# Where the key and value loads of a decode kernel land: a turning ring of eighteen slots against two whole-head places

## The chip, the cores and the metric

The kernel runs on one core of one Trainium2 chip. The metric is device time in microseconds (us) of one execution, lower is better. The kernel before takes 1354.32 us (median of 3 runs, 1352.16 to 1354.4). The trace that is read here is of one more execution, whose own time was 1351.85 us; from its first to its last instruction the profile counts a span of 1349.9 us.

Five engines work beside each other: TensorE (PE in the profile, its weight loads PEld), VectorE (DVE), ScalarE (ACT), GpSimd (POOL) and SyncE (SP). SP does no arithmetic here; it issues the transfers of keys and values. ACT issues those of most weights. A transfer is carried out by 16 DMA engines, and a transfer of 128 rows gives each of them eight packets and then a short one that tells the semaphore.

## The reference: one token, two layers, a long cache

The same weights and the same cache serve both layers. Everything is float32.

```python
# x: 1 x 640; k_cache, v_cache: 32 heads x 8192 x 128; wq: 640 x 4096; wo: 4096 x 640
# w1: 640 x 1728; w2: 1728 x 640
x = x + attention(layernorm(x))   # q = x wq; p = softmax(q k^T / sqrt(128)); (p v) wo
x = x + relu(layernorm(x) w1) w2
x = x + attention(layernorm(x))
x = x + relu(layernorm(x) w1) w2
```

There is one query, so each layer reads the whole cache: 32 heads of 8 MB (4 MB of keys and 4 MB of values), and does little with each byte.

## The kernel before: heads in a row, a ring for their loads

**The ring.** One tile, `ring`, holds whatever of the cache is on the chip: `RING` = 4760 units of 32 bytes in each of the 128 partitions, 4 KB over all of them. A piece of keys (a quarter of a head's keys, `K_ALL`) or of values (`V_ALL`) takes 256 units, which is 1 MB. A head is four pieces of keys and four of values: 2048 units, 8 MB. Head 0 has nine, since its last piece of values is cut in halves, so that little work is left when the last one lands.

**The list of loads.** `todo` is a list of (layer, unit, first piece, piece behind the last, place), written when the program is built. `pump` (called at the start, and by `release` after each piece has been used) takes loads from its head in order, as long as the place wanted is free of live pieces (`is_free`), or, where no place is given, as long as `place` finds a gap that fits. Each load is one `nc.sync.dma_start` (L210). So all loads of keys and values stand in one line on SP: a load that waits for its place holds up those behind it, and on the chip SP waits until TensorE has read the last old piece that the new load covers.

**Places.** In the first layer heads run from 0 to 31, in the second from 31 to 0. Some pieces of heads 29 to 31 stay on the chip from the first layer to the second (`KEPT` = 3960 units) and are not loaded twice. Heads 2 to 26 (`FULL`) are stored as one unit of keys and values. `turning` walks them around 18 slots of 256 units (`SLOTS`): a head takes the next eight slots, and where the ring of 18 ends within a head, the head is loaded in two loads, one up to the end and one from slot 0. Of its 48 heads (25 in the first layer, 23 in the second) 31 are whole and 17 divided: 2 and 6 slots, 4 and 4, or 6 and 2. The other loads have their own cuts: in the first layer head 0 is six loads and head 1 four; in the second layer heads 26 and 25 are two each (keys, values), head 1 four, head 0 six. The four blocks of `w2` come last in each layer, through `place`.

**The work of a head.** `scores` (L454) multiplies the query with the key pieces on TensorE, 32 matmul records a head; `row_maxima` (L465, DVE) and `exponentials` (L470 PE, L477 DVE, L479 ACT exp, L483 and L485 DVE) make the weights, and `values` (L503) multiplies them with the value pieces, 32 records again. `output` (L518 to L533) sums the rows. Each piece is released as soon as its own matmuls are done, so keys are free some 7 us before values. In between lie side jobs: the next group's queries (L393 to L417), the projection with `wo` (L425), the folding of the last `wo` rows into `w1` (L569 to L604). In the second layer the first three heads are interleaved (`AHEAD`). TensorE takes everything in the written order: a head's matmuls wait for its pieces and hold up the next head's.

**The end of a layer.** Before the last head's values are done, the rest is projected (`before_last`) and the first part of the MLP (`hidden`, L609) runs between its pieces; then come the sums (L547), the last part of `hidden`, the turn of its result (L825 to L841) and the product with `w2` (L425 within `times_rows`).

The functions as the diff touches them:

Of the kernel before, what the change touches and what calls it, by code (L numbers as in the profile page):

```python
# [17 lines left out]
H = 32  # L18
# [15 lines left out]
RUN = COLS // 4  # L34
NBL = RUN // P
K_ALL = [(r, 0, RUN) for r in range(4)]
V_ALL = [(b, 0, 4) for b in range(NBL)]
WHOLE = [("k", K_ALL), ("v", V_ALL)]
HALVES = [("k", K_ALL[:2]), ("k", K_ALL[2:]), ("v", V_ALL[:2]), ("v", V_ALL[2:])]
LAST = [("v", V_ALL[:2]), ("v", V_ALL[2:3]), ("v", [(3, 0, 2)]), ("v", [(3, 2, 2)])]  # L40
FULL = range(2, 27)
UNITS = {h: [("kv", K_ALL + V_ALL)] if h in FULL else WHOLE for h in range(H)}
UNITS[0] = HALVES[:2] + LAST
UNITS[1] = HALVES
UNITS[28] = HALVES
UNITS[29] = [
    ("k", K_ALL[:1]),
# [9 lines left out]
]  # L57
UNITS[30] = [
    ("k", [(0, 432, 80), (1, 0, 80)]),
    ("k", [(0, 0, 432)]),  # L60
    ("k", [(1, 80, 432)] + K_ALL[2:]),
] + HALVES[2:]
UNITS[31] = HALVES[:2] + LAST
DROPPED = {29: 9, 30: 2}
# [3 lines left out]
AHEAD = 3  # L68


SLOT = RUN // 2
SLOTS = 18


def kind_of(unit, t):

    return unit[0] if unit[0] != "kv" else "k" if t < len(K_ALL) else "v"


def wide(kind, piece):  # L80

    if kind == "w":
        return D // 8
    return 4 * piece[2] * (1 if kind == "k" else DH) // 8
# [13 lines left out]
W2_ALL = [("w2", i) for i in range(len(W2_RUNS))]  # L98
# [4 lines left out]
def decode_kernel(ctx: ExitStack, tc: tile.TileContext, x, kv, wq, wo, w1, w2, w2_rest, out):  # L103
# [15 lines left out]
    kept = [u for u in order if u[0] >= min(DROPPED) and u[1] >= DROPPED.get(u[0], 0)]  # L119
# [3 lines left out]
    todo = []  # L123

    def all_of(layer, u):
        todo.append((layer, u, 0, len(UNITS[u[0]][u[1]][1]), None))

    def turning(layer, heads, slot):

        for h in heads:  # L130
            a, end = 0, len(UNITS[h][0][1])
            while a < end:
                b = min(end, a + SLOTS - slot)
                todo.append((layer, (h, 0), a, b, SLOT * slot))
                slot = (slot + b - a) % SLOTS
                a = b

    for h in range(H):
        if h == FULL[0]:
            turning(0, FULL, 16)  # L140
        if h not in FULL:
            for i in range(len(UNITS[h])):
                all_of(0, (h, i))
    for u in W2_ALL:
        all_of(0, u)
    for h in range(H)[::-1]:
        if h == FULL[-1]:
            todo.append((1, (h, 0), 0, len(K_ALL), None))
            todo.append((1, (h, 0), len(K_ALL), len(K_ALL) + len(V_ALL), None))
            h = FULL[-2]  # L150
            todo.append((1, (h, 0), 0, len(K_ALL), 0))
            todo.append((1, (h, 0), len(K_ALL), len(K_ALL) + len(V_ALL), SLOT * len(K_ALL)))
            turning(1, FULL[:-2][::-1], 8)
        if h not in FULL and h != 30:
            for i in range(len(UNITS[h])):
                if (h, i) not in kept:
                    all_of(1, (h, i))
    for u in W2_ALL:
        all_of(1, u)
    source = {}  # L160
    for us, dram in ((order, kv), (W2_ALL, w2)):
        o = 0
# [7 lines left out]
    def place(layer, u, n):  # L170

        step = 512 if n % 512 == 0 else 8
        if layer:
            low, high = 0, RING
        elif u[0] in range(FULL[0]):
            low, high = 0, 16 * SLOT
        elif u[0] == "w2":
            low, high = KEPT, RING
        elif u in apart:
            low, high = apart[u]  # L180
        else:
            low, high = 0, 3072
        at, best = low, None
        for a, m in sorted(live.values()) + [(high, 0)]:
            a = min(a, high)
            for base in (0, 3328, KEPT):
                c = base + -(-max(at - base, 0) // step) * step
                if a - c >= n and (best is None or a - at < best[1]):
                    best = c, a - at
            at = max(at, a + m)  # L190
        return None if best is None else best[0]
# [4 lines left out]
    def pump():  # L196
        while todo:
            layer, u, first, last, at = todo[0]
            unit = UNITS[u[0]][u[1]]
            ns = [wide(kind_of(unit, t), piece) for t, piece in enumerate(unit[1])]  # L200
            n = sum(ns[first:last])
            if at is None:
                at = place(layer, u, n)
                if at is None:
                    return
            elif not is_free(at, n):
                return
            todo.pop(0)
            o = 8 * sum(ns[:first])
            nc.sync.dma_start(ring[:, 8 * at : 8 * (at + n)], source[u][:, o : o + 8 * n])  # L210
            for t in range(first, last):
                live[layer, u, t] = at, ns[t]
                at_of[layer, u, t] = ring, 8 * at
                at += ns[t]
# [759 lines left out]
```

## Time and profile before

| what | value |
|---|---|
| median of 3 runs | 1354.32 us (1352.16 to 1354.4) |
| the profiled execution's own time | 1351.85 us |
| its span, first to last instruction | 1349.9 us |
| PE busy | 787.8 us (58%) |
| DVE busy | 251.6 us (19%) |
| ACT busy | 59.1 us (4%) |
| bytes moved by DMA | 574.52 MB, 426 GB/s over the span |
| loads of keys and values with no size shown | 31 |

Busy time of an engine is the union of its instructions. The DMA share is the mean busy share of the 16 DMA engines. "us to landing" of a load runs from its issue on SP until all 16 engines have told its semaphore, so it includes the time in which the load stood behind earlier ones. The chain of waits is followed back from the last instruction: at each step to what released it.

### The profile page before, as it was taken

What the parts mean: (1) busy time and instruction counts of PE and PEld (TensorE: products, weight loads), DVE (VectorE), ACT (ScalarE), POOL (GpSimd) and SP (SyncE); (2) the same over time, 40 slices, a digit from 0 to 9 for tenths busy, and PEclk for the clock granted to TensorE, in tenths of its full rate; (3) what the DMA queues carried; (4) which work ended last, traced back from release to release, by engine and by line L of the source; (5) the groups of instructions that cost most, each with busy time, mean ns of one, the idle gap of its engine ahead of it and who ended that gap; (6) DMA issues with size and microseconds to landing.
All of it is one profiled execution on the core that took longest, in us unless ns stands there. A gap on an engine that the chain in (4) does not pass through costs nothing.

```text
span 1349.9 us, 13614 instructions
## 1 busy us (share of the span) xinstructions
PE 787.8 (58%) x6080; PEld 268.6 (20%) x6080; DVE 251.6 (19%) x794; ACT 59.1 (4%) x149; POOL 2.9 (0%) x10
## 2 busy tenths in 40 slices
PE   5454555554755655566588664575466554665658
PEld 2011111111211211121143211122122121211214
DVE  2111111221211211122122211122111111112212
ACT  0000000000000000000000000000000000000000
POOL 0000000000000000000000000000000000000000
PEclk8677677868878876789799877788778778878879
DMA  9999999999999999999999999999999999999997
GB/s 395 438 428 441 423 430 442 425 427 430 439 429 429 432 434 422 447 416 420 426 382 425 435 430 438 424 436 429 436 435 427 426 438 429 434 421 438 429 422 317
DMA packets 25409, 574.52 MB, mean 426 GB/s; under 512 B 2820, under 2 KB 2952, under 8 KB 6024
## 3 DMA queue, kind: packets, MB, share of 16 engines
q1 hardware_dynamic: 20600, 531.15, 91.7%
q10 hardware_dynamic: 4752, 42.52, 7.5%
q8 instruction: 47, 0.77, 0.2%
q14 instruction: 10, 0.08, 0.0%
HBM read 573.65 MB, written 0.00 MB: 425 GB/s over the span
## 4 chain that ended last, share of the span: by engine, by line
DMA 66%; PE 27%; DVE 5%; issue 1%; ACT 1%; ACTq 0%; SPq 0%; DVEq 0%
DMA ring<-in_kv 65%; PE ps L454 13%; PE outs L503 8%; DVE h_t L465 2%; PE px L393 1%; DVE pt L483 1%; PE pm L470 1%; ACT p L479 1%; DVE p L522 1%; PE acc L425 0%; PE px L425 0%; PE acc L609 0%; PE px L408 0%; DVE pT L485 0%; DMA ring<-in_w 0%
## 5 line engine op out<-in xcount | busy, mean ns | idle before, releaser
L454 PE MATMUL ps<-ring,spread_q 128*32 128x512 f32 (+3 forms) x2104 | 326.2, 767 | 337.7 <-DMA ring<-in_kv 332.4
L503 PE MATMUL outs<-ring,pT 128*4 128x512 f32 (+1 forms) x2080 | 260.6, 642 | 32.8 <-DVE pT L485 17.5
L454 PEld LDWEIGHTS ps<-ring,spread_q 128*32 128x32 f32 x2104 | 76.2, 137 | 523.2 <-issue 298.9
L465 DVE TENSOR_REDUCE h_t<-ps 128x1 f32<-128x512 f32 x64 | 44.3, 692 | 637.1 <-PE ps L454 637.1
L479 ACT ACTIVATE p<-ps,h_t 128x512 f32<-128x512 f32 x64 | 44.0, 687 | 1227.3 <-DVE h_t L477 1207.6
L503 PEld LDWEIGHTS outs<-ring,pT 128*4 128x4 f32 x2080 | 51.6, 91 | 181.8 <-issue 149.4
L532 PE MATMUL pm<-ones,p 128*128 128x1 f32 x120 | 23.2, 262 | 94.9 <-DVE p L522 94.9
L518 DVE TENSOR_SCALAR p<-outs,ind 128x128 f32<-128x128 f32 x60 | 21.1, 351 | 246.4 <-PE outs L503 246.4
L522 DVE SCALAR_TENSOR_TENSOR p<-outs,ind,p 128x128 f32<-128x128 f32 x180 | 63.1, 351 | 6.4
L483 DVE STREAM_TRANSPOSE pt<-p 128x512 f32<-128x512 f32 x64 | 46.5, 727 | 58.2 <-ACT p L479 58.2
L470 PE MATMUL pm<-row_of,h_t 128*128 128x16 f32 x128 | 26.3, 281 | 50.0 <-DVE h_t L465 49.0
L532 PEld LDWEIGHTS pm<-ones,p 128*128 128x128 f32 x120 | 18.0, 190 | 152.1 <-DVE p L522 150.8
L470 PEld LDWEIGHTS pm<-row_of,h_t 128*128 128x128 f32 x128 | 20.0, 196 | 110.1 <-DVE h_t L465 108.2
L596 PE MATMUL px<-w_t,wct 128*128 128x448 f32 (+1 forms) x80 | 35.1, 553 | 1.1 <-ACT wct L589 1.1
L393 PE MATMUL px<-wq_t,ln_xc 128*32 128x256 f32 x280 | 34.3, 393 | 0.0
L492 PE MATMUL pm<-ind,h_t 128*128 128x1 f32 x128 | 22.6, 246 | 15.3 <-ACT p L479 15.3
L492 PEld LDWEIGHTS pm<-ind,h_t 128*128 128x128 f32 x128 | 22.1, 198 | 33.3 <-ACT p L479 27.0
L425 PE MATMUL acc<-wo_t,o_cols 128*32 128x160 f32 x496 | 21.5, 313 | 0.6 <-DVE o_cols L550 0.6
L533 DVE TENSOR_SCALAR o_cols<-pm,h_t 128x1 f32<-128x1 f32 x60 | 13.1, 219 | 30.5 <-PE pm L532 30.5
L393 PEld LDWEIGHTS px<-wq_t,ln_xc 128*32 128x32 f32 x280 | 15.7, 113 | 13.7 <-issue 2.9
L477 DVE TENSOR_REDUCE h_t<-pm 128x1 f32<-128x16 f32 x64 | 11.2, 175 | 33.1 <-PE pm L470 33.1
L425 PEld LDWEIGHTS acc<-wo_t,o_cols 128*32 128x32 f32 x496 | 15.0, 113 | 3.9 <-issue 1.5
(110 smaller groups left out, 203.4 us busy)
## 6 DMA issues: line engine op xcount, KB each, us to landing
ring<-in_kv SPq DMA_DIRECT2D x20, 4096.0 KB, 35.5
ring<-in_kv SPq DMA_DIRECT2D x38, 2048.0 KB, 28.5
ring<-in_kv SPq DMA_DIRECT2D x11, 6144.0 KB, 37.7
wq_t<-in_wq ACTq DMA_DIRECT2D x14, 1280.0 KB, 25.0
wo_t<-in_wo ACTq DMA_DIRECT2D x14, 1280.0 KB, 25.6
ring<-in_kv SPq DMA_DIRECT2D x15, 1024.0 KB, 12.7
ring<-in_w SPq DMA_DIRECT2D x4, 1280.0 KB, 26.9
w_t<-in_w ACTq DMA_DIRECT2D x1, 4320.0 KB, 49.3
```

The costliest lines, as they stand in the source:

```text
L393: nc.tensor.matmul(pq[32 * j : 32 * j + 32, :n], xc[:, c : c + 1].to_broadcast([P, 32]), wq_t[g][:, c, j * n : (j + 1) * n], start=(c == 0 ...
L425: nc.tensor.matmul(acc[32 * g : 32 * g + 32, :DR], col.to_broadcast([col.shape[0], 32]), wt[:, g * DR : (g + 1) * DR], start=first, stop=last,
L454: nc.tensor.matmul(hd.ps[32 * g : 32 * g + 32, c : c + n], spread_q[:, 3 - r : 35 - r], tile_of[:, at + g * n : at + (g + 1) * n], start=f ...
L465: nc.vector.tensor_reduce(hd.nm, hd.ps, AX.X, ALU.max, negate=True)
L470: nc.tensor.matmul(pt[:, :16], hd.nm.to_broadcast([P, P]), row_of.rearrange("p g r -> p (g r)"), start=True, stop=True,)
L479: nc.scalar.activation(hd.p, hd.ps, AF.Exp, bias=hd.low, scale=1.0, accum_out=hd.l)
L483: nc.vector.transpose(pt, hd.p)
L492: nc.tensor.matmul(pt[:, :1], hd.l.to_broadcast([P, P]), ind[:, 4:5], start=True, stop=True)
L503: nc.tensor.matmul(hd.out[32 * g : 32 * g + 4, r : r + m].rearrange("p r d -> p (r d)"), hd.pT[:, 4 * i : 4 * i + 4], tile_of[:, v : v + m ...
L522: nc.vector.scalar_tensor_tensor(oc[:, r], hd.out[:, r], ind[:, r : r + 1], oc[:, r - 1], op0=ALU.mult, op1=ALU.add,)
L532: nc.tensor.matmul(pt[:, :1], oc[:, 3], ones, start=True, stop=True)
L596: nc.tensor.matmul(pt[:, :n], wct[:, c], w1_t[:, c, f : f + n], start=(c == 0), stop=(c == NB - 1),)
```

## The change: two places, whole heads

Heads 0 to 26 become one unit each. `turning` and the 18 slots go. `parts_of` gives a head one of two places of 2048 units: the first layer's even heads have place 0 and its odd heads place 2048, the second layer's odd heads place 0 and its even heads place 2048 (head 26 of the second layer goes wherever `place` finds room, as before). A head is one load, except where `PARTS` cuts it: head 0 of the first layer as keys, then values; in the second layer heads 26, 25 and 2 as keys, then values, head 1 in four loads and head 0 in six. Loads of heads 27 to 31 and of `w2` are listed as before, but their places are found among other live pieces. Units 4096 to 4760 hold nothing of heads 2 to 26 any more. What the engines compute, and in which order, stays the same: the pieces are the same and are used in the same order.

```diff
-UNITS = {h: [("kv", K_ALL + V_ALL)] if h in FULL else WHOLE for h in range(H)}
-UNITS[0] = HALVES[:2] + LAST
-UNITS[1] = HALVES
+UNITS = {h: [("kv", K_ALL + V_ALL)] if h <= FULL[-1] else WHOLE for h in range(H)}
+UNITS[0] = [("kv", K_ALL + V_ALL[:3] + [(3, 0, 2), (3, 2, 2)])]
+PARTS = [{0: [4, 9]}, {26: [4, 8], 25: [4, 8], 2: [4, 8], 1: [2, 4, 6, 8], 0: [2, 4, 6, 7, 8, 9]}]
...
-SLOT = RUN // 2
-SLOTS = 18
+HALF = 4 * RUN
...
-    def turning(layer, heads, slot):
-
-        for h in heads:
-            a, end = 0, len(UNITS[h][0][1])
-            while a < end:
-                b = min(end, a + SLOTS - slot)
-                todo.append((layer, (h, 0), a, b, SLOT * slot))
-                slot = (slot + b - a) % SLOTS
-                a = b
...
+    def parts_of(layer, h):
+
+        ((kind, pieces),) = UNITS[h]
+        ns = [wide(kind_of((kind, pieces), t), piece) for t, piece in enumerate(pieces)]
+        at = None if (layer, h) == (1, FULL[-1]) else HALF * (h % 2 != layer)
+        a = 0
+        for b in PARTS[layer].get(h, [len(pieces)]):
+            todo.append((layer, (h, 0), a, b, at))
+            if at is not None:
+                at += sum(ns[a:b])
+            a = b
+
+    for layer in range(2):
+        for h in range(H)[:: 1 - 2 * layer]:
+            if h <= FULL[-1]:
+                parts_of(layer, h)
+            elif not layer or h != 30:
+                for i in range(len(UNITS[h])):
+                    if not layer or (h, i) not in kept:
+                        all_of(layer, (h, i))
+        for u in W2_ALL:
+            all_of(layer, u)
...
-        elif u[0] in range(FULL[0]):
-            low, high = 0, 16 * SLOT
```

More of the change, by code (lines that the diff above doesn't have):

```diff
@@ L126, in all_of @@
         todo.append((layer, u, 0, len(UNITS[u[0]][u[1]][1]), None))
-    def turning(layer, heads, slot):
-        for h in heads:
-            a, end = 0, len(UNITS[h][0][1])
-            while a < end:
-                b = min(end, a + SLOTS - slot)
-                todo.append((layer, (h, 0), a, b, SLOT * slot))
-                slot = (slot + b - a) % SLOTS
-                a = b
[L138 to L159, printed above, removed]
+    def parts_of(layer, h):
[18 more added lines that the diff above has]
+            all_of(layer, u)
     source = {}
```

## The prediction, made before the changed kernel had run

> **What bounds the kernel now.** I read the page's lines on DMA first, then the busy time in the two long stretches between the layers' ends, then the chain of waits.
>
> ```profile
> span 1349.9 us, 13614 instructions
> ...
> DMA  9999999999999999999999999999999999999997
> ...
> q1 hardware_dynamic: 20600, 531.15, 91.7%
> q10 hardware_dynamic: 4752, 42.52, 7.5%
> ...
> DMA 66%; PE 27%; DVE 5%; issue 1%; ACT 1%; ACTq 0%; SPq 0%; DVEq 0%
> ```
>
> ```profile
> 30.00:670.00 640.00, 357.24 (x2582) 114.25 (x2574) 113.22 (x341) 25.48 (x64) 0.00 (x0) 0.78 1.00 430
> 725.00:1325.00 600.00, 346.99 (x2596) 115.26 (x2592) 113.56 (x344) 26.63 (x67) 0.00 (x0) 0.82 1.00 431
> ```
>
> The second fence's columns are the stretch, its length, busy time (count) of PE, PEld, DVE, ACT and POOL, the granted clock, the DMA share and GB/s. For 1240 of the 1349.9 us the DMA engines have a share of 1.00. PE works little over half of that time. So in the long stretches nothing can be won by loading earlier. What is left is the time that a byte takes on the DMA engines, and the places where something else sets the end.
>
> One such place is the end of the kernel, seen in the chain of waits:
>
> ```profile
> 1266.69 28.31 DMA ring<-in_kv
> 1295.00 0.04 issue
> 1295.05 5.82 PE ps L454 x32
> ...
> 1304.19 3.66 PE outs L503 x32
> ...
> 1317.31 3.66 PE outs L503 x32
> ...
> 1336.06 0.92 PE outs L503 x14
> 1336.98 0.02 issue
> ...
> 1347.35 0.01 DVEq L968
> ```
>
> The last landing on the chain is that of the second layer's head 2, whole, at 1295.00. From there 52 us of PE, DVE and ACT follow: heads 2, 1 and 0, then the MLP. The loads behind head 2 land before they are wanted.
>
> **Fewer loads.** The groups of DMA issues show today's sizes; whole heads are the 31 for which no size is given.
>
> ```profile
> ring<-in_kv SPq DMA_DIRECT2D x20, 4096.0 KB, 35.5
> ring<-in_kv SPq DMA_DIRECT2D x38, 2048.0 KB, 28.5
> ring<-in_kv SPq DMA_DIRECT2D x11, 6144.0 KB, 37.7
> ...
> ring<-in_kv SPq DMA_DIRECT2D x31, 31.9
> ```
>
> By the lists, heads 0 to 26 are 6 + 4 + 34 = 44 loads in the first layer today and 2 + 26 = 28 after. In the second they are 2 + 2 + 31 + 4 + 6 = 45 and then 2 + 2 + 22 + 2 + 4 + 6 = 38. That is 16 and 7 loads fewer, 23 in all, with the same bytes. What does one more load cost where the DMA engines are full? Two places without weight loads tell, the chain of waits in the second layer and TensorE's timeline of the first layer's head 1:
>
> ```profile
> 756.47 36.34 DMA ring<-in_kv
> ...
> 798.31 33.27 DMA ring<-in_kv
> ```
>
> ```profile
> 35.71 3.64 PE L454 MATMUL ps<-ring,spread_q 128*32 128x512 f32 x16 [1.92 <-DMA ring<-in_kv]
> 40.60 1.92 PE L454 MATMUL ps<-ring,spread_q 128*32 128x512 f32 x16 [1.25 <-DMA ring<-in_kv]
> 45.89 2.85 PE L503 MATMUL outs<-ring,pT 128*4 128x512 f32 x16 [0.64 <-DVE pT L485]
> 50.39 3.43 PE L503 MATMUL outs<-ring,pT 128*4 128x512 f32 x16 [1.65 <-DMA ring<-in_kv]
> ```
>
> From 792.81 (756.47 + 36.34) to 831.58 (798.31 + 33.27) land head 25 in two loads and head 24 in one: 16 MB and 3 loads in 38.77 us. From 35.71 to 50.39, where PE starts on landings, come 6 MB in 3 loads: 14.68 us. With b us for a MB and a for a load, 16b + 3a = 38.77 and 6b + 3a = 14.68, so b = 2.409 and a = 0.075 us. The page gives a second, rougher reading: q1's share is 0.917 x 16 x 1349.9 = 19806 engine-us for 20600 packets and 531.15 MB, q10's 1620 for 4752 and 42.52; the two solve to 0.011 us a packet, and a load has nine per engine, so 0.10 us. I take 0.075, since landings include what overlaps, with 0.05 and 0.10 as ends. 23 loads are 1.73 us (1.2 to 2.3): 1.2 before the first layer's end, 0.5 in the second.
>
> The Trainium skill, "DMA: Bandwidth & Descriptors", section "Measured (HBM→SBUF, 128 partitions, SWDGE, issued from GpSimd)", gives about 10.5 ns a packet, for another way of issuing. Nine packets a load and 23 loads would be 2.2 us by it; the landings say 1.73 and decide.
>
> **Less room ahead.** Today a load of 2 to 6 slots can go while the head before last is still in work, since 18 slots are 2.25 heads, and a head that crosses no end waits only for the last old piece under its slots. With two places head h+2 goes when the last values of head h are read, and then only head h+1 stands in the queue. It takes 38.77 / 2 = 19.4 us. The queue runs dry if head h's work and the start of a load together take longer. The slow heads are those with side jobs or a low clock; head 7 of the first layer is one, in PE's timeline:
>
> ```profile
> 188.00 6.33 PE L454 MATMUL ps<-ring,spread_q 128*32 128x512 f32 x32 [10.21 <-DMA ring<-in_kv]
> ...
> 197.71 6.57 PE L503 MATMUL outs<-ring,pT 128*4 128x512 f32 x32 [0.59 <-DVE pT L485]
> ```
>
> From landing to the last value matmul that is 204.28 - 188.00 = 16.3 us. How long a load takes from its issue to its first bytes isn't shown, but a bound is, since a small load (320 KB, itself under 0.8 us at 2.4 us a MB) lands so soon after its issue:
>
> ```profile
> wct<-in_kv SPq DMA_DIRECT2D x1, 320.0 KB, 2.9
> ```
>
> 16.3 + 2.9 = 19.2 us, under 19.4, and the heads with side jobs are also those beside which 1280 KB weight loads run, which lengthen the cover by some 3 us each. So the cost here is nothing; what hides it is head h+1's transfer, and without that cover a load would cost up to 2.9 us of gap each. SP has nothing else behind these waits but later loads of the ring: weights go through ACT's queue. Head 0, as keys then values, holds its place until its values are done, some 3 us later than today, while head 1's 19.4 us run.
>
> The thinnest cover is moved, not made: the second layer's head 25 today gets its keys in when head 27's scores are done, and after the change when head 26's are, at 788.98, which is when its values go today.
>
> ```profile
> 788.98 10.14 SPq L210 DMA_DIRECT2D ring<-in_kv  x3
> ```
>
> What stands before it lands at 792.81: 3.8 us, above the bound of 2.9. At the first layer's end head 27's values likewise wait for head 26's scores, with head 27's keys in the queue (9.7 us). Nothing again.
>
> **Head 2 as keys, then values.** Its keys will land some 9.7 us before its values, so scores and exponentials run beside the values' transfer, and after the landing near 1295 only 3.66 us of value matmuls are left instead of the 12.8 us to 1307.85. The chain at the end gets 9 us of slack, far more than it can use: the loads of heads 1 and 0 become what is late next. How much that gives, the landings of head 0 say:
>
> ```profile
> 1298.75 0.33 SPq L210 DMA_DIRECT2D ring<-in_kv  x1
> ```
>
> ```profile
> ring<-in_kv SPq DMA_DIRECT2D x1, 2048.0 KB, 26.4
> ```
>
> ```profile
> 1306.20 0.38 SPq L210 DMA_DIRECT2D ring<-in_kv  x1
> ```
>
> ```profile
> ring<-in_kv SPq DMA_DIRECT2D x1, 512.0 KB, 29.3
> ```
>
> The second half of its keys lands at 1325.15 and the last piece of values at 1335.5. The first layer's end is already paced by these same loads, and shows the way from keys to the end of the values:
>
> ```profile
> 660.26 22.56 DMA ring<-in_kv
> ...
> 692.41 1.04 PE outs L503 x16
> ```
>
> That is 682.82 to 693.45, 10.6 us. In the second layer, with everything 1.73 us earlier: keys 1323.4, so values done at 1334.05; the last values land at 1333.8 and need some 0.5 us, 1334.3. The later holds, rounded to 1334.5 for waits between. Today it is 1336.98. **Sum:** 1336.98 - 1334.5 = 2.5 us at the end, which contains the 1.73 of the loads; 0.8 is the chain's share. The span goes from 1349.9 to 1347.4 and the profiled execution from 1351.85 to 1349.35. That execution was 2.5 us under the median of the runs, so against 1354.32 the forecast is **1351.8 us**. Own range: 1.2 to 3.7 less, 1350.6 to 1353.1.
>
> **The rivals.** *The clock falls at the end, so that only little is won.* Paced by loads, PE works and waits by turns. Against it: the first layer's end, paced the same way, keeps the clock at 1.00. For it: head 1's start in the first layer, also fed by 2048 KB loads, has 0.72, and 16 matmuls took 1.92 us at one place and 3.43 to 3.64 at others.
>
> ```profile
> 676.00:694.00 18.00, 15.35 (x154) 5.98 (x147) 3.67 (x12) 1.17 (x4) 0.00 (x0) 1.00 1.00 418
> ...
> 36.00:55.00 19.00, 12.34 (x68) 2.21 (x60) 2.99 (x9) 0.78 (x2) 0.00 (x0) 0.72 1.00 426
> ```
>
> Slow keys and values of head 0 add 1.7 us for the last two key pieces, and about as much again until PE has worked for a while: 2 us off the gain, 1353.8 us. The Trainium skill, "TensorE: Matmul & The Clock Gate", section "HAM oscillation — how this bites in real kernels", has the clock halved after PE gaps of more than about 3.4 us, which speaks against this change; the gaps of 1.25 and 1.65 us above stand beside slow matmuls already, so the trace is, if anything, harsher.
>
> *More is won.* Were a load 0.10 us (2.3 in all) and the values' end bound by landings alone, 1.4 us more: 3.7 less, 1350.6 us. The page's rounder reading speaks for it, the landings against.
>
> *The queue runs dry* (the slower side). If the heads with side jobs, one in four of 52, took head 1's 18.1 us (35.71 to 53.82, its waits for pieces included) and a load's start its whole 2.9, each would leave 21.0 - 19.4 = 1.6 us empty: 13 x 1.6 = 21 us, 1373 us. It decides from 16.5 us of work on. Against it: 16.3 is the longest I found among whole heads, and weight loads run then.
>
> *It doesn't do what it says*: head 2's keys wait for its old place longer than the queue lasts, so no split is felt: 1.73 less, 1352.6. Head 4's scores free it some 19 us ahead; unlikely.
>
> **How the numbers follow.** Forecast 0.43; clock 0.27; more 0.12; dry 0.13; no effect of the split 0.05. A measurement tells about 0.2%, 2.7 us, from no change. The forecast lies at 0.19%, so half of it, with nearly all of "more" and a little besides, is faster: 0.38. The other half, the clock case and the last make 0.47; dry makes most of 0.15. The range goes from 1349.3 (more, and 1.3 for the scatter of medians) to 1357.0, which takes in the clock case with a colder end and a queue that runs dry by 0.4 us a time.
>
> **What would show it.** The DMA share must stay at 1.00 from 30 to 670 and from 725 to 1325; q1 must have 23 x 144 = 3312 packets fewer, about 17290. Whole heads' landings must be 19.4 us apart where no weights run. The chain at the end must go through a landing of head 0, not head 2, and the clock from 1320 on must be 1.00. A share under 0.99, or PE waits for landings longer than 19.4 us behind SP waits for values, would make me wrong on the side of slower.

## The result and the profile after

| | before | changed |
|---|---|---|
| median | 1353.63 us (1351.57 to 1356.14, 22 executions) | 1357.32 us (1350.53 to 1362.27, 22) |
| ratio | 1 | 1.0023 (95%: 1.0013 to 1.0033) |
| the profiled execution, its span | 1351.85, 1349.9 us | 1353.79, 1352.0 us |

The change costs 3.7 us where 2.5 were to be won. The changed kernel also scatters more than twice as far (11.7 us from the lowest to the highest against 4.6), and its profiled execution is one of the quick ones. So a second profile of it is read beside the first: "run again", with a span of 1355.3 us, near its median.

The first view is the page of the changed kernel, by its lines on DMA and on the chain of waits.

```profile
span 1352.0 us, 13576 instructions
...
DMA  9999999999999999999999999999999999999997
...
q1 hardware_dynamic: 17288, 531.15, 91.6%
q10 hardware_dynamic: 4752, 42.52, 7.5%
...
DMA 66%; PE 28%; DVE 4%; issue 1%; ACT 1%; SPq 0%; ACTq 0%; DVEq 0%
```

The loads are those announced: 3312 packets fewer, the same bytes. The long stretches are as full as before, seen in the windows of the changed kernel (stretch, length, busy time and count of PE, PEld, DVE, ACT and POOL, granted clock, DMA share, GB/s):

```profile
30.00:670.00 640.00, 365.95 (x2610) 117.72 (x2602) 113.67 (x342) 26.13 (x66) 0.00 (x0) 0.79 1.00 430
725.00:1325.00 600.00, 362.09 (x2590) 117.56 (x2590) 114.59 (x348) 26.63 (x67) 0.00 (x0) 0.81 1.00 430
```

Against 430 and 431 GB/s of before, that is one to two us of 600 (1/431 of it is 1.4). What differs lies at the layers' ends. The chain of waits of the changed kernel, run again:

```profile
1286.05 29.14 DMA ring<-in_kv
1315.19 0.04 issue
1315.24 3.60 PE outs L490 x16
...
1323.31 1.86 PE ps L441 x8
...
1326.65 2.94 PE ps L441 x14
...
1337.16 0.92 PE outs L490 x14
...
1342.95 1.11 PE px L412 x14
1344.06 0.52 PE pm L326 x2
1344.58 3.67 PE px L412 x48
1348.25 0.52 PE pm L339 x2
1348.77 3.40 PE px L412 x48
...
1352.65 0.01 DVEq L955
```

The same end in the kernel before, where the prediction's rows have the last values done at 1336.98 and the end at 1347.35:

```profile
1341.77 0.57 PE px L425 x14
1342.34 0.37 PE pm L339 x2
1342.70 2.04 PE px L425 x48
1344.74 0.31 PE pm L352 x2
1345.06 1.81 PE px L425 x48
```

The chain now goes through a landing of head 1, not of head 2. From there PE runs at about half its speed of before in three stretches: the second half of head 1's values (16 matmuls in 3.60 us, where 32 took 3.66), head 0's keys (8 and 14 matmuls in 1.86 and 2.94 us, where the chain of before has 1.00 and 1.77), and everything from 1342.5 on. The last values in between keep their speed, 0.92 us. The last value matmul is done at 1338.08 instead of 1336.98 (1.1 us later), and from there to the end it takes 14.57 us instead of 10.37 (4.2 us). Together that is the 5.4 us between the spans, to 0.1. I call this last part, the sums, the last part of `hidden`, the turn and the product with `w2`, the **tail**. In the first profile of the changed kernel the tail kept its speed (1338.99 to 1349.35), but the product with `w2` at the first layer's end did not, 3.67 and 3.40 us again:

```profile
699.23 3.67 PE px L412 x48
...
703.41 3.40 PE px L412 x48
```

So the question was why the clock falls at the layers' ends, and which part of the change makes it fall. Two theories were put to the chip. **Theory A, the refill:** two places leave the DMA engines dry at times, and the loads come late. **Theory B, the clock:** with head 2 divided, PE waits between landings before heads 1 and 0, and the granted clock falls there.

### The profile page after: what moved, and what is told of

Its sections match the earlier page's. It is cut to its first block, busy times and chain, and to the rows that moved or that the text cites. A ratio compares the mean times of both kernels' runs of the same rounds, so it can differ in the third digit from the quotient of the medians.

```text
span 1352.0 us, 13576 instructions
## 1 busy us (share of the span) xinstructions
PE 809.6 (60%) x6080; PEld 274.9 (20%) x6080; DVE 251.6 (19%) x794; ACT 59.1 (4%) x149; POOL 2.9 (0%) x10
## 3 DMA queue, kind: packets, MB, share of 16 engines
q1 hardware_dynamic: 17288, 531.15, 91.6%
## 4 chain that ended last, share of the span: by engine, by line
DMA 66%; PE 28%; DVE 4%; issue 1%; ACT 1%; SPq 0%; ACTq 0%; DVEq 0%
DMA ring<-in_kv 66%; PE ps L441 13%; PE outs L490 9%; DVE h_t L452 2%; PE px L380 1%; PE pm L457 1%; PE px L412 1%; DVE pt L470 1%; PE acc L412 1%; ACT p L466 1%; PE px L583 1%; PE acc L596 0%; PE px L395 0%; DVE pT L472 0%; PE pm L479 0%
## 5 line engine op out<-in xcount | busy, mean ns | idle before, releaser
L441 PE MATMUL ps<-ring,spread_q 128*32 128x512 f32 (+3 forms) x2104 | 342.3, 804 | 318.2 <-DMA ring<-in_kv 313.3
L490 PE MATMUL outs<-ring,pT 128*4 128x512 f32 (+1 forms) x2080 | 264.8, 651 | 33.1 <-DVE pT L472 18.2
L441 PEld LDWEIGHTS ps<-ring,spread_q 128*32 128x32 f32 x2104 | 81.5, 144 | 518.8 <-issue 340.4
L457 PEld LDWEIGHTS pm<-row_of,h_t 128*128 128x128 f32 x128 | 19.4, 190 | 106.5 <-DVE h_t L452 104.6
```

What stands on the lines that cost most here:

```text
L441: nc.tensor.matmul(hd.ps[32 * g : 32 * g + 32, c : c + n], spread_q[:, 3 - r : 35 - r], tile_of[:, at + g * n : at + (g + 1) * n], start=f ...
L457: nc.tensor.matmul(pt[:, :16], hd.nm.to_broadcast([P, P]), row_of.rearrange("p g r -> p (g r)"), start=True, stop=True,)
L490: nc.tensor.matmul(hd.out[32 * g : 32 * g + 4, r : r + m].rearrange("p r d -> p (r d)"), hd.pT[:, 4 * i : 4 * i + 4], tile_of[:, v : v + m ...
```

## The experiments

Ratios are to the kernel before on the same chip, with their 95% intervals. The filling and extra matmuls below go into a scratch bank that nothing reads.

### The changed kernel again, more cuts, and head 2's split alone

The changed kernel without an edit:

> The changed kernel once more, on the chip that times the next three. Theory A (refill): with two places a load goes only when the last values of the head before last are read; the DMA engines that are ahead of the others have by then run dry, and each such place costs idle time and slow first packets that are not won back. Theory B (clock): the ends of the layers run at a lower granted clock because TensorE waits between landings. Both expect a median some 3 to 4 us over the kernel before and a wider scatter. A expects the DMA engines' active count to fall in several places between 30 and 1325 us, 1 to 3 us of idle time in all; B expects a full DMA there and a granted clock under 0.9 from 690 to 705 or in the last 25 us.

Every head cut in its place, behind the fourth or the sixth piece, with the second place kept:

```diff
 PARTS = [{0: [4, 9]}, {26: [4, 8], 25: [4, 8], 2: [4, 8], ...
+for layer in range(2):
+    for h in range(1 + layer, 27):
+        PARTS[layer].setdefault(h, [4, 8])    # the other run: [6, 8]
```

> The changed kernel with each head from 1 on in two loads, keys and values, in the same places, so that the next load of a place goes some 7 us earlier (after the keys are scored). 47 loads more than the changed kernel: 47 x 0.075 = 3.5 us if each load costs what landings of the kernel before say. A: no dry places are left, so about 1351.8 + 3.5 = 1355.3, 2 us under the changed kernel, and its scatter falls back to that of the kernel before. B: the clock at the ends is as it was, 1357.3 + 3.5 = 1360.8.

> The same with the cut behind the sixth piece, so that 6 MB of a head's 8 go 1.8 us earlier than in the changed kernel, as early in a head's work as the kernel before lets most of its whole heads go. The loads are as many as with the cut behind the keys. A: most dry places go, 1355 to 1357. B: 1360.8. If both cuts measure alike, 1.8 us of cover is all that the old ring had and the new places lack.

The kernel before with nothing of the change but head 2 in two loads:

```diff
             b = min(end, a + SLOTS - slot)
+            if (layer, h) == (1, 2):
+                b = min(b, a + len(K_ALL))
```

> The kernel before with one edit: the second layer's head 2 in two loads, keys and values, in the slots it has. By the prediction's step the end of the kernel comes 0.8 us earlier, less 0.075 for the load: ratio 0.9995. B: nothing is won, since TensorE waits more and its clock falls at the end: 1.000 or up to 1 us more.

| run | median, us | ratio |
|---|---|---|
| changed, again | 1356.91 | 1.0028 (1.0014 to 1.0041) |
| cut behind the fourth piece | 1355.83 | 1.0017 (1.0005 to 1.0030) |
| cut behind the sixth piece | 1358.69 | 1.0032 (1.0018 to 1.0047) |
| before, head 2 divided | 1355.90 | 1.0017 (1.0004 to 1.0030) |

The medians of the two cuts don't decide. 1355.83 us is near A's 1355.3, and 1358.69 lies between A's 1355 to 1357 and B's 1360.8; both intervals overlap that of the changed kernel. The traces say more. The changed kernel run again shows both signs: between the layers' ends the DMA engines were idle for 1.1 us in the mean of the 16, and in the last 25 us the clock was 0.80. With the cut behind the fourth piece the idle time is 0.15 us, and the way from the last value matmul to the end takes 14.62 us all the same. That speaks against A as the main cause. The last run speaks for B: one more load, in the kernel before, without the two places and with no idle time of the DMA engines, costs 2.3 us (0.0017 x 1353.4), where 1 us was expected at most, and has the same slow tail in its chain of waits:

```profile
1337.28 0.92 PE outs L505 x14
...
1344.75 3.67 PE px L427 x48
...
1348.93 3.40 PE px L427 x48
```

### Each half of the change alone

The changed kernel with head 2 in one load:

```diff
-PARTS = [{0: [4, 9]}, {26: [4, 8], 25: [4, 8], 2: [4, 8], 1: [2, 4, 6, 8], ...
+PARTS = [{0: [4, 9]}, {26: [4, 8], 25: [4, 8], 1: [2, 4, 6, 8], ...
```

> The changed kernel with the second layer's head 2 in one load again, as in the kernel before; all else as changed. Theory B (the split lets TensorE wait for landings behind head 2, the clock falls, and the work after the last landing runs slower): head 2, 1 and 0 follow each other without waits again, from the last value matmul to the end it takes 10.4 us as in the kernel before and not 14.6, and the 22 loads fewer show: 1353.4 - 22 x 0.075 = 1351.8. Theory A (the refill of two places): as the changed kernel, 1356 to 1357.

Two places in the first layer only; the second layer's list as in the kernel before:

```diff
     for h in range(H):
-        if h == FULL[0]:
-            turning(0, FULL, 16)
-        if h not in FULL:
+        if h <= FULL[-1]:
+            parts_of(0, h)
+        else:
...
+    parts_of(1, 26)
+    parts_of(1, 25)
+    turning(1, FULL[:-2][::-1], 8)
+    cut(1, 1, [2, 4, 6, 8])
+    cut(1, 0, [2, 4, 6, 7, 8, 9])
```

> Two whole-head places in the first layer alone, with its heads 0 and 1 in long loads; the second layer's loads are cut and placed as in the kernel before. 16 loads fewer. B: 1353.4 - 1.2 = 1352.2. A: the first layer's share of dry places, about half of the changed kernel's loss: 1354.5 to 1355.5.

Measured: 1353.25 us, ratio **0.9998** (0.9987 to 1.0008), and 1353.48 us, **0.9992** (0.9982 to 1.0003). B's 1351.8 and 1352.2 were not reached: the loads saved (24 in the first run, not 22) don't show clearly. But without the split the changed kernel is as quick as the one before, and the tail is back, here in the chain of the run with head 2 in one load:

```profile
1338.29 0.92 PE outs L490 x14
...
1344.93 2.04 PE px L412 x48
...
1347.28 1.81 PE px L412 x48
```

### Keeping PE busy between the landings

Three matmuls of 128x512 after every second piece of the second layer's head 1 and after head 0's second piece of keys, in the changed kernel and in the one with head 2 in one load:

```diff
+                    if near_end and L and hd.scored % 2 == 0:
+                        keep_busy(3)
...
+                if near_end and L and a % 2:
+                    keep_busy(3)
...
         next_scores(hd)
+        if L:
+            keep_busy(3)
```

> The changed kernel, head 2 cut as changed, with three extra matmuls on old data (some 1.3 us at full clock) at each of five places in the second layer's heads 1 and 0, behind every second piece of keys or values of head 1 and behind head 0's second piece of keys, so that TensorE has less idle time there. They compute nothing that is used. B: the clock stays at 1.0 from 1300 us on, the work behind the last value matmul takes 10.4 us, 1352 to 1353. A: 1356 to 1357, or more by the extra matmuls.

> Both: head 2 in one load and the extra matmuls. B: nothing to mend is left, so like the kernel with head 2 whole, 1351 to 1352, if the extra matmuls stand in waits; where heads 1 and 0 come without waits they cost up to 5 x 1.3 us of TensorE time on the chain, 1356 or so. A: 1357 or more.

Measured: 1362.68 us, 1.0070 (1.0053 to 1.0088), and 1369.50 us, 1.0121 (1.0102 to 1.0139). The matmuls were dearer than the waits that they were to fill, in PE's timeline of the first of the two:

```profile
1305.61 3.49 PE L346 MATMUL px<-w_t 128*128 128x512 f32 x6
```

Three take 3.49 us, not the 1.3 that I had reckoned. The runs tell only that: with five such groups the heads became PE's own work. In the first one the clock stayed at 1.00 from 1300 us to the last values, and the tail took 14.6 us all the same, where B had expected 10.4. This moved the question from the waits to the tail itself.

### Filling the tail

The stretch of small sums behind the last value matmul gets more to do for the matmul array, in both layers:

```diff
         rows = copied_rows(hd)
-        keep_busy(1, 128)
+        keep_busy(1, 256)
         o = work.tile([P, 1], F32, name="c_ol")
         summed_rows(hd, rows, o)
+        keep_busy(1, 128)
...
         times_rows(pd, wo_t[last // HG][:, last % HG], o, True, True)
-        keep_busy(1, 128)
+        keep_busy(1, 256)
```

> The changed kernel with more filling work in the stretch of small sums behind each layer's last value matmul: the two matmuls on old data there work on 256 columns and not 128, and a third of 128 columns stands behind the sums of the last head. They compute nothing that is used, and cost some 0.3 to 0.7 us on the chain of each layer if the clock is the same. Theory B, sharpened (the head 2 that is cut makes TensorE wait before head 0, which locks the last stretch to the windows of the clock gate so that one window falls into the small sums, and the w2 product then runs at half clock): the time from the last value matmul to the end falls from 14.6 to about 11 us, and the median from 1357 to 1354. If the sums are not what lowers the clock: 14.6 and more, 1357.5.

> The same filling work in the kernel before, whose clock mostly stays up there. B: a little slower by the work itself in executions that kept the clock, faster in those that lost it at either layer's end: 1353 to 1354.5, with less scatter (the kernel before spreads over 4 us).

Changed: 1353.39 us, **0.9993** (0.9983 to 1.0004), against 1.0023 and 1.0028 without it. Before: 1352.85 us, 1.0006 (0.9990 to 1.0023); two of its twelve executions took 1360.7 and 1361.2 us, where less scatter had been expected, and make that interval wide. PE's timeline and the windows of the changed kernel with the tail filled:

```profile
1336.51 0.70 PE L346 MATMUL px<-w_t 128*128 128x256 f32 x2
...
1338.06 0.47 PE L346 MATMUL px<-w_t 128*128 128x128 f32 x2
```

```profile
1336.60:1342.40 5.80, 5.68 (x66) 4.03 (x70) 2.01 (x10) 0.74 (x3) 0.00 (x0) 1.00 0.90 374
1342.40:1347.10 4.70, 4.13 (x99) 2.95 (x98) 1.35 (x7) 0.00 (x0) 0.55 (x1) 1.00 0.15 58
```

Some 1 us of matmuls that compute nothing wanted keeps the clock at 1.00 to the end and brings 4 us back.

The same filling work at the second layer's end alone, in the changed kernel (each count as above `if L`, else as before):

> The changed kernel with the filling work at the second layer's end alone. With it at both ends the ratio was 0.9993, without it 1.0023 to 1.0028. If the loss lies in the second layer's end alone, this run is at 0.999 to 1.000 like the one with both; if half of it lies at the first layer's end, it is at 1.0005 to 1.0015.

1353.17 us, **0.9994** (0.9984 to 1.0005): the same as with both. So what the changed kernel loses, it loses at the second layer's end, to within the intervals of 0.1%.

And the filling work beside the split in the kernel before, beside the changed kernel with head 2 in one load, and beside two places in the first layer alone:

> The kernel before with one thing of the change alone, the second layer's head 2 as keys, then values, and with three small matmul groups as filling work in the stretch of small sums at each layer's end. The split alone measured 1.0017. If what the split costs is only the clock lost in that stretch (14.6 in place of 10.4 us behind the last value matmul), the stretch is back at about 10.5 us and the split's own gain of 0.8 us shows: 0.9988 to 0.9998. If the split costs by its waits before head 1 and head 0 as such, the ratio stays at 1.001 to 1.002.

> The changed kernel with head 2 in one load, and the filling work at both layers' ends. Without the filling work it measured 0.9998. The clock at the second layer's end was never lost there, so the filling work can save time only at the first layer's end, where the clock was 0.89 between 690 and 705 us: 1 to 2 us by the theory of the clock, ratio 0.9985 to 0.9995. If the refill of two places is what holds it at 1, the ratio stays at 0.9998.

> Two places in the first layer only, the second layer loaded as before, and the filling work at both ends. Without filling work 0.9992, with a first layer's end that lost the clock (19.3 us from the last value of head 31 to the next layer's first scores, against 15.6 to 17). By the theory of the clock 1 to 2 us less: 0.998 to 0.999, the best of all versions. By the theory of the refill no change: 0.9992.

| run | without filling | with filling |
|---|---|---|
| before, head 2 divided | 1.0017 (1.0004 to 1.0030) | 0.9987 (0.9973 to 1.0002) |
| changed | 1.0028 (1.0014 to 1.0041) | 0.9993 (0.9983 to 1.0004) |
| changed, head 2 in one load | 0.9998 (0.9987 to 1.0008) | 0.9986 (0.9975 to 0.9996) |
| two places in the first layer alone | 0.9992 (0.9982 to 1.0003) | 0.9984 (0.9974 to 0.9995) |

The split kernels come back by 0.30 and 0.35%, clear of their intervals. The other two gain 0.12 and 0.08%, which the intervals don't settle. The last two, at 1352.54 and 1352.36 us, are the versions whose intervals lie below the kernel before, and so below the changed one. Whether two places add anything to the filling work isn't settled, since the filled kernel before is known so roughly.

The split kernel before, with its tail filled, in the chain of waits:

```profile
1339.27 0.86 PE outs L505 x16
...
1345.98 2.04 PE px L427 x48
...
1348.33 1.81 PE px L427 x48
```

### Longer heads, to see the refill by itself

Two matmuls of 128x512, some 2.3 us, ahead of the sums of 38 heads, with two places (head 2 in one load) and in the kernel before:

```diff
+            if h in FULL and (L or where > 13):
+                keep_busy(2, 512, "pt")
             total(hd)
```

> The kernel with two places and head 2 whole, with two matmuls on old data (some 2.3 us) put into 38 of its heads ahead of the value matmuls, so that a place comes free 2.3 us later. Theory A (engines that run dry cost): the cover of 19.4 us is used up but for some 3 us, and each of these heads leaves idle DMA time in the records; several us slower than without, 1357 or more. If only the last of the 16 engines counts, as the prediction had it: nothing, 1353 to 1354.

> The same filling work in the kernel before, where most loads wait for a head's sixth piece and not its last, 1.8 us earlier. A: 1354 to 1355, little, since this much more is covered. If only the last engine counts: nothing. If extra work on TensorE costs by itself, as much as in the kernel with two places.

Two places: 1362.10 us, 1.0068 (1.0056 to 1.0080). Before: 1358.41 us, 1.0038 (1.0026 to 1.0050). The windows of the one and of the other:

```profile
725.00:1325.00 600.00, 398.77 (x2610) 129.34 (x2614) 112.22 (x336) 25.48 (x64) 0.00 (x0) 0.82 1.00 425
```

```profile
725.00:1325.00 600.00, 396.16 (x2644) 129.01 (x2648) 114.20 (x342) 26.26 (x66) 0.00 (x0) 0.84 1.00 430
```

PE's work is nearly the same, the bytes are not: 5 of 430 GB/s is 7 us of the 600. From head 26's first scores to head 2's it takes 518.75 us with two places and 511.74 with the ring. The two profiles overstate it, since the one is the slowest of its five executions and the other the quickest of its five; the medians lie 3.7 us apart. So Theory A names something real, which the changed kernel escapes but for a small part. The 4.9 us that the kernel before loses lie elsewhere, most of them after head 2's start, where PE sets the end: 55.98 us from there to the end instead of 52.31.

## Why the prediction was wrong

**What bounds the kernel** held: share 1.00, 430 GB/s, and heads 19.3 us apart where no weights run, as in these two starts of scores in PE's timeline of the changed kernel:

```profile
1002.61 6.03 PE L441 MATMUL ps<-ring,spread_q 128*32 128x512 f32 x32 [4.92 <-DMA ring<-in_kv]
1021.86 4.95 PE L441 MATMUL ps<-ring,spread_q 128*32 128x512 f32 x32 [2.68 <-DMA ring<-in_kv]
```

**Fewer loads:** the counts were right (17288 packets, about 17290 forecast), the price roughly. With ten loads more than the kernel before in the first layer, the two runs with cuts end its last transfer of values at 692.65 and 692.68 us, against 691.95 in the mean of five profiles with the ring (691.65 to 692.31): 0.07 us a load, from two profiles. But 16 fewer end it at 691.55 in the mean of ten profiles (690.63 to 692.20): 0.4 us, where 1.2 were booked. And the changed kernel with head 2 in one load, 24 loads fewer (17144 packets), differs from the kernel before by -0.3 us (-1.8 to +1.1), where 24 x 0.075 would be 1.8. The two cuts add 47 loads to the changed kernel, 3.5 us at the booked price, and the medians moved by -1.1 and +1.8 us. So by the first layer's transfers the term brought a third of its size; the interval of the medians still holds the whole of it. (The rival "more is won" has a slip in its sum: 2.5 and 1.4 us are 3.9, not 3.7. Neither came.)

**Less room ahead, cost nothing:** nearly. Without the extra work the DMA engines' idle time between the layers' ends, in the mean of the 16, was 0.26 and 1.34 us in the first profile of the changed kernel and 0.77 and 0.36 in the second, against 0.00 and 0.07 before. One such place, SP's timeline and the windows around it:

```profile
1187.59 0.33 SPq L197 DMA_DIRECT2D ring<-in_kv  x1
```

```profile
1185.00:1187.00 2.00, 2.00 (x24) 0.43 (x16) 0.00 (x0) 0.00 (x0) 0.00 (x0) 1.00 1.06 459
1187.50:1189.00 1.50, 0.03 (x4) 0.00 (x0) 1.29 (x4) 0.00 (x0) 0.00 (x0) 1.00 1.14 393
1189.00:1192.00 3.00, 0.45 (x6) 0.36 (x10) 0.33 (x2) 0.00 (x0) 0.00 (x0) 0.97 1.06 437
```

The load went only when the last values of its place had been read, and some engines had run out. The share doesn't show it, since it counts a packet whole in the window where the packet starts; by the packets' own starts and ends, 5 of the 16 engines were at work at 1188.5. These 1.1 to 1.6 us are about what the loads' term lost; that the one is eaten by the other fits, and no run separates them. The rival "the queue runs dry", with its 16.5 us of work as the point from which it decides, was sound as a mechanism: with 2.3 us more work in 38 heads, two places cost 0.30% (4 us) more than the ring does. It wasn't what happened.

**Head 2 as keys, then values: this step failed**, and with it the sign. Its first half came true: head 2 is done early, and head 1's and head 0's loads are late next. That they are late is the loss. The step booked 1334.5 for the last value matmul and nothing for a slower way from there to the end. Run again, the changed kernel has 1338.08, 3.6 us later than booked, and then a tail that is 4.2 us longer. Two signs named beforehand failed with it: the chain goes through a landing of head 1 and not of head 0, and the clock from 1320 on isn't 1.00. Its path from head 0's keys to the end of the values, 10.6 us, was read at the first layer's end, at full clock. PE's timeline of the changed kernel, run again, shows the wait for head 1's second half of values, and the matmuls behind it:

```profile
1310.75 1.90 PE L490 MATMUL outs<-ring,pT 128*4 128x512 f32 x16 [0.64 <-DVE pT L472]
1315.24 3.55 PE L490 MATMUL outs<-ring,pT 128*4 128x512 f32 x16 [2.58 <-DMA ring<-in_kv]
```

In the kernel before these 32 matmuls ran through without a wait, since head 2 had kept PE behind its loads:

```profile
1317.31 3.62 PE L503 MATMUL outs<-ring,pT 128*4 128x512 f32 x32 [0.64 <-DVE pT L485]
```

Taking the split out of the changed kernel brings the ratio from 1.0023 and 1.0028 to 0.9998, 3.4 to 4.1 us: all that was lost. The slack of 9 us at head 2 was cover: it kept PE busy while head 1 and head 0 landed. From there to the end the clock goes up and down in steps of 3.41 us. The windows of the changed kernel, run again, cut at those steps:

```profile
1308.40:1311.80 3.40, 2.58 (x18) 0.94 (x21) 1.27 (x5) 0.78 (x2) 0.00 (x0) 1.00 0.99 419
1311.80:1315.20 3.40, 0.85 (x8) 0.00 (x0) 0.00 (x0) 0.00 (x0) 0.00 (x0) 1.00 1.02 434
1315.20:1318.60 3.40, 3.36 (x16) 0.41 (x16) 0.00 (x0) 0.00 (x0) 0.00 (x0) 0.50 0.99 419
1318.60:1322.00 3.40, 2.53 (x29) 1.41 (x25) 0.98 (x4) 0.37 (x1) 0.00 (x0) 1.00 1.04 443
1322.00:1328.80 6.80, 6.80 (x44) 2.81 (x44) 0.38 (x2) 0.00 (x0) 0.00 (x0) 0.50 0.98 412
1328.90:1342.50 13.60, 11.98 (x121) 5.78 (x114) 3.44 (x11) 1.52 (x5) 0.00 (x0) 1.00 0.91 375
1342.50:1352.70 10.20, 9.62 (x124) 5.93 (x124) 1.80 (x11) 0.00 (x0) 0.55 (x1) 0.50 0.02 9
```

What PE does in a window sets the clock of the next. PE busy for 0.85 of 3.40 us: the next at half speed. Busy for 3.36: back to full. Where small sums stand, the busy time alone doesn't tell: the window from 1318.60 is busy for 2.53 us, the first of the two from 1322.00 for all of its time, and behind both the clock is at half, so that head 0's keys take 1.86 and 2.94 us. Before the last fall, at 1342.50, PE had small sums too, and the fall covers the whole product with `w2`.

**The rival "the clock falls at the end"** named the mechanism, with 0.27 and 2 us. Its size was wrong. It counted the slow keys and values of head 0 and stopped at the last value matmul; the 4.2 us of the tail were in no case. Of the two gaps that it set beside slow matmuls, the one of 1.25 us stands before 16 matmuls of 1.92 us, which is full speed. Of the six profiles of kernels with head 2 divided and the tail unfilled, five have a longer tail (14.6 us in four, 11.8 in one) and the first of the changed kernel has 10.4. The six with head 2 in one load and the tail unfilled all have 10.4, and the six with the tail filled all have 10.5, whether head 2 is divided or not.

**What stays open:** why the fall in the tail comes with the split so regularly. When it comes, the clock's records in the traces show. The steps of 3.41 us run through the whole profile, and what counts is where one of them stands behind the last value matmul. Of the twelve profiles with the tail unfilled, the five that lost the clock in the tail are those with a step 0.8 to 1.1 us behind it: the window that begins there holds the small sums, and the next is at half speed. In the other seven the first step stands at 0.0, 1.4 or 2.2 to 3.4 us, and the clock holds; the first profile of the changed kernel is one of them. With the tail filled it held with steps at 0.7 and 0.9 us as well.

Why the split brings a step to that place so often is the open part. In four of the five the clock last rises at a step within head 0's keys, and the time at full clock between that rise and the fall is 13.65 us, four steps. The work in between takes the same time each time, so the steps may fall on the same sums; in the other kernels they would fall anywhere. The fifth is the run with the extra matmuls, whose clock was full from 1300 on and had no such rise. It was not tried by itself. Whether the split gains its 0.8 us of the chain once the clock is kept stays open too: 0.9987 (0.9973 to 1.0002) allows it, and in the changed kernel with the tail filled it shows nothing (0.9993 with, 0.9986 without). Last, the stretch from head 31's last values to the next layer's first scores took 15.6 to 19.4 us from one profile to another, of kernels with the ring and with two places alike. It goes with the clock: over that stretch the clock was 1.00 in the five profiles with 15.6 to 16.5 us and 0.74 to 0.90 in all the others. The run with head 2 in one load and the tail filled, with 19.0 us, kept it at 1.00 up to 706.4 and had 0.50 from there; PE waited 1.99 us for the last block of `w2`, where the changed kernel run again, with 15.6 us, waited 0.31, and 40 matmuls of the next layer's queries took 2.36 us instead of 1.30. This is some of the scatter of all the times.

## What to carry to other kernels

Slack on a chain at the end can be cover: ask what the engine does in the time that it no longer works, before the slack is given to its loads. Where an engine's speed depends on how busy it was, follow the chain to the last instruction at both speeds, through the small operations too; here the largest term lay behind the place at which the prediction stopped. And a few matmuls into a scratch bank, in the stretch of small sums, brought back what the split had cost.

## What the runs showed of the hardware

**When the clock falls and rises.** I cut six profiles from 20 to 1345 us (before, changed, changed again, head 2 in one load, two places in the first layer, head 2 divided alone) at the clock's steps, into windows of 3.413 us, and took PE's busy share in each and the clock in the next:

| clock in the window | PE busy in it | windows | next at full clock |
|---|---|---|---|
| full | under 0.40 | 276 | 0 |
| full | over 0.62 | 861 | 849 |
| half | under 0.70 | 480 | 0 |
| half | 0.90 and more | 353 | 343 |

The fall lies near half a window (at a share of 0.48 to 0.51 38% stay, at 0.51 to 0.54 83%), the return, less sharply, between 0.75 and 0.9. The 12 windows that were busy and lost the clock all begin at the layers' ends, from 692.9 to 704.3 and from 1318.6 to 1339.2 us, where much of PE's time goes into small sums. That products of one to four columns count for little, though the profile has PE as busy, is my reading; the filled tails fit it, and so do the places of the steps in the unfilled ones. The Trainium skill, "TensorE: Matmul & The Clock Gate", section "HAM oscillation — how this bites in real kernels", asks for no idle gaps of PE over about 3.4 us. The trace agrees on the length of the window, and is harsher on the gap: 2.58 us of waiting within one window were enough, and in the tail no gap was needed.

**What a wait for a place costs the queue.** The load issued at 1187.59 had its first packets under way 1.0 us later and the engines busy again about 1.5 us later, and those first packets took up to 3.26 us instead of the usual 2.42. So the prediction's bound of 2.9 us for a load's start was about twice too long here.
